# One kernel, another deal of side work: gate rounds 3-2-3, sums of magnitudes moved, weight-block sums split

## The chip, the core and the metric

The kernel runs on one core of a Trainium2 chip. The metric is the device time of one execution in microseconds (us). Five engines work side by side, each on its own in-order queue: TensorE (PE in the profile, with PEld for its weight loads) multiplies, VectorE (DVE), ScalarE (ACT) and GpSimd (POOL) do elementwise work, SyncE (SP) issues the DMAs. An instruction waits for semaphores of other engines, and all behind it on its queue wait with it.

## What is computed

Attention with a learned position bias, a gated feed-forward layer over its output, and then a layer of eight experts, whose part is the one that changes:

```python
def _moe2_ref(x, w_gate, w1, w2):           # x 1152x512, w1 8x512x1024, w2 8x1024x512
    logits = x @ w_gate
    P = np.exp(logits - logits.max())
    for _ in range(8):                       # the gate rounds
        P /= P.sum(1, keepdims=True) + 1e-09 # rows
        P /= P.sum(0, keepdims=True) + 1e-09 # columns
        P *= N / E
    for e in range(E):
        h = np.maximum(x @ w1[e], 0.0)       # first products
        out += P[:, e:e + 1] * (h @ w2[e])   # second products
```

## The kernel before

All products run in 16 bits with each operand split into a high and a low part; three products of parts make one. To split, a weight block is scaled by a power of two that comes from its largest magnitude ("sums of magnitudes", lines 754 on DVE and 102 on ACT; they go to DRAM and back, are read by line 751, and lines 727 to 836 make the power).

**First products.** `up(n, extra)` for n = 0 to 31, four blocks per expert, computes a block of `h` by seven products (x, z, y, x, y, x, z: the order of PSUM tiles, a Strassen-like scheme) of twelve matmuls each (line 1241). ACT copies a result out (`snap`, line 1251), DVE joins (lines 1255, 1300), ACT makes the high part of `h` (line 1259), DVE the low part (line 1264). Between the products are seven places, "segments" 0 to 6, where `then(seg)` runs side work that `between` or `extra` hold for (n, seg).

**Side work.** `prep(n, k)` makes weight block n ready for `up(n)`: step 0 scales (line 931, ACT), 1 and 2 make sums of blocks (lines 935, 936 and 939, 940, DVE), 3 and 4 the high parts (lines 943 and 947, ACT) and 3 and 5 the low parts (lines 944 and 950, POOL). `p2(e, i)` splits a row block of `w2[e]`: for e = 0, first four, lines 1032 (ACT) and 1033 (DVE), later lines 1035, 1036 (ACT) and 1037 (POOL). `pe(e, i)` takes one magnitude of expert e, `send` and `power` carry it on. `t4` makes sums of `w2` blocks (line 1325).

**Second products.** The first expert uses `down_0(h)`, once for each half of its `h` (after n = 2 and n = 4): nine tiles of 128 tokens, twelve matmuls each (line 1344), into `ps_d`, a PSUM pool of two buffers; `add` takes the result to `acc`, on ACT in the first half (line 1333), on DVE in the second (line 1335). Experts 1 to 7 use `down(e)` after their fourth block: half of tile 8, four rounds i = 0 to 3 on a pair of tiles each, by seven products of sums (lines 1419, 1424), the rest of tile 8. DVE makes the sums of `h` for the next round (line 1412) and accumulates (line 1335). Side work of a round stands in a table by (i, place); place 3 is ahead of the accumulations of `pz`, place 4 behind that of `py`.

**Gate.** `gate` takes the logits; `top` and `spread` find the largest and spread it to all lanes (`nmx`, line 1162), then ACT takes the exponential. A round is `rows` (lines 1169 to 1172, DVE) and `cols` (a matmul, line 1176, and lines 1177 to 1180 on DVE). The eight rounds lie in the first expert, one column sum after another.

The order is written out by hand: each engine's queue follows the order of calls in the program, and pools of buffers set the waits.

Of the kernel before, what the change touches and what calls it, by code (L numbers as in the profile page):

```python
# [52 lines left out]
def make_body(stop=None):  # L53
    def body(tc, a):
# [21 lines left out]
        with ctx, tc.manual_schedule():  # L76
# [146 lines left out]
            with ExitStack() as bctx:  # L223
# [180 lines left out]
                for g16 in range(NG16):  # L404
                    ps = bias_mm(g16)
                    t = bias_ev(g16, ps)
# [415 lines left out]
            def peak_all(name, items):  # L822

                items = [x for x in items if x[0] < 2 * NE]
                if items:
                    m = scl.tile([128, 2], F32, tag="pm", name="pm", bufs=2)[:, 0:len(items)]
                    peak_in(name, m)
                    peak_pow(m, items)
# [273 lines left out]
            with ExitStack() as ectx:  # L1102
# [44 lines left out]
                def gate():  # L1147
                    V.tensor_copy(out=P.rearrange("p t e -> p (t e)"), in_=pg[0][:, :NTT * NE])
                    mx = sk.tile([128, 1], F32, name="mx")
                    V.tensor_reduce(out=mx, in_=P, op=ALU.max, axis=AX.XY)  # L1150
                    nm = sk.tile([1, 1], F32, name="nm")
                    nmx = sk.tile([128, 1], F32, name="nmx")

                    def top():
                        pm = ps_d.tile([128, 512], F32, tag="d", name="pm")
                        T.transpose(pm[:1, :128], mx, ident)
                        V.tensor_reduce(out=nm, in_=pm[:1, :128], op=ALU.max, axis=AX.X, negate=True)

                    def spread():
                        pm2 = ps_d.tile([128, 512], F32, tag="d", name="pm2")  # L1160
                        T.matmul(out=pm2[:, 0:1], lhsT=ones[:1, :], rhs=nm, start=True, stop=True)
                        V.tensor_copy(out=nmx, in_=pm2[:, 0:1])
                        A.activation(out=P, in_=P, func=AF.Exp, bias=nmx)

                    between[2, 4].insert(0, top)
                    between[2, 6].append(spread)

                def rows():
                    V.tensor_reduce(out=row, in_=P, op=ALU.add, axis=AX.X)
# [25 lines left out]
                def m_spread():  # L1195
# [7 lines left out]

                between = {(0, 0): [m_top, end("t2"), end("h4")], (0, 1): [end("l4"), end("l2v"), end("tb")],
                           (0, 2): [end("t4"), end("h5"), end("l5")], (0, 3): [end("h6"), end("l6")],
                           (1, 5): [p2(0)], (2, 0): [lambda: peak_all(*SC), p2(1)], (2, 4): [p2(3)], (2, 5): [],
                           (1, 6): [logits], (2, 2): [flip], (2, 3): [gate, p2(2)], (1, 2): [lambda: peak_get(SC[0])],
                           (2, 6): []}
                kh_t = {}

# [157 lines left out]
                def down_0(h):  # L1368

                    parts = [(*h_t.pop(h), *w2t[0], 4 * h)]  # L1370
                    kh = kh_t.pop(h)
                    jp.append(sn)
                    if h == 0:
                        todo = {0: p2(0, 4) + pe(1, 1, 2, 3) + send(1, 1), 1: p2(0, 5), 2: prep(3, 1), 3: prep(3, 2, 3) + p2(0, 6),
                                4: p2(0, 7) + pe(1, 4, 5), 5: prep(3, 4, 5) + pe(1, 6), 6: power(1, 1) + prep(4, 0),
                                7: prep(4, 1, 3) + pe(1, 7), 8: prep(4, 2) + pe(1, 8, 9)}
                    else:
                        todo = {0: power(1, 2) + prep(5, 0), 1: prep(5, 1, 2) + p2(1, 0), 2: prep(5, 3) + p2(1, 1),
                                3: prep(5, 4, 5) + pe(2, 0) + p2(1, 2), 4: p2(1, 3) + prep(6, 0), 5: prep(6, 1) + p2(1, 4),
                                6: prep(6, 2, 3) + p2(1, 5), 7: pe(2, 1) + p2(1, 6) + pe(2, 4), 8: p2(1, 7) + pe(2, 5)}  # L1380
                    for t in range(NTT):
                        add(t, slice(0, DM), next(plain(t, parts)), kh, h, h == 0)
                        if h == 0 and t in (2, 4, 6, 8) or h == 1 and t in (0, 4):
                            cols(banks[0])
                        if t == 0 or h == 0 and t in (2, 4, 6, 8):
                            rows()
                        run(todo.get(t, ()))
                    jp.pop()

                def down(e):  # L1390
# [38 lines left out]
                    if e < NE - 1:  # L1429
                        put(0, 3, power(e + 1, 2) + [lambda: pace(e + 1)] + p2(e + 1, 0, 1, 2, 3))  # L1430
                        put(1, 0, power(e + 1, 1))
                        for i in range(3):
                            put(i + 1, 0, prep(4 * e + 4 + i, 0))
                            put(i + 1, 3, prep(4 * e + 4 + i, 1, 2, 4, 5, 3) + p2(e + 1, *((4,), (5,), (6, 7))[i]))
                        put(2, 1, pe(e + 2, 4, 5))
                        put(2, 2, pe(e + 2, 6, 7))
                        put(3, 1, pe(e + 2, 8))
# [58 lines left out]
                for n in range(4 * NE):  # L1496
                    e, q = divmod(n, 4)
                    extra = {}
                    put = lambda seg, fs: extra.setdefault(seg, []).extend(fs)
                    if n == 1:  # L1500
                        for seg, ks in ((0, (0,)), (1, (1, 2)), (2, (3,)), (3, (4, 5))):
                            put(seg, prep(2, *ks))
                    if n == 2:
                        put(3, prep(3, 0))
                    if n == 1:
                        put(6, pe(1, 0))
                    if n == 3:
                        put(0, prep(4, 4, 5) + pe(1, 10))
                        put(1, pe(1, 11))
                        put(2, send(1, 2))  # L1510
                    if n == 4:
                        for seg in (1, 5):
                            put(seg, [lambda: cols(ps_d)])
                            put(seg + 1, [rows])
                    if n in (2, 4):
                        put(3, [lambda h=n // 2 - 1: gains(h)])
                    if e and q == (1 if e == 1 else 0):
                        b_s = split_b(e)
                    t4 = lambda *ks: [b_s[k] for k in ks]
                    if n == 5:  # L1520
                        put(0, prep(6, 4, 5) + pe(2, 6))
                        put(1, pe(2, 2))
                        put(2, t4(0))
                        put(3, prep(7, 0))
                        put(4, prep(7, 1))
                        put(5, pe(2, 7))
                        put(6, prep(7, 2))
                    if n == 6:
                        put(0, prep(7, 3, 4, 5))
                        put(1, pe(2, 3))  # L1530
                        put(2, t4(1))
                        put(3, pe(2, 8, 9))
                        put(4, t4(2))
                        put(6, t4(3))
                    if n == 7:
                        put(0, pe(2, 10, 11) + t4(4))
                        put(1, [lambda: send_both(2)] + t4(5, 6))
                        put(2, t4(7))
                    if e > 1:
                        if q == 0:  # L1540
                            put(0, pe(e + 1, 9))
                            put(1, pe(e + 1, 0))
                            put(2, t4(0))
                            put(3, prep(n + 3, 0))
                            put(4, t4(1))
                            put(6, t4(2))
                        if q == 1:
                            put(0, prep(n + 2, 3) + pe(e + 1, 10))
                            put(1, pe(e + 1, 1))
                            put(2, prep(n + 2, 1))  # L1550
                            put(4, prep(n + 2, 2))
                            put(6, t4(3))
                        if q == 2:
                            put(0, prep(n + 1, 4, 5) + pe(e + 1, 11))
                            put(1, send(e + 1, 2) + pe(e + 1, 2))
                            put(2, t4(4))
                            put(4, t4(5))
                        if q == 3:
                            put(1, pe(e + 1, 3))
                            put(2, send(e + 1, 1) + t4(6))  # L1560
                            put(4, t4(7))
                    if e and q == 3:
                        put(4, [lambda: gains(e + 1)])
                    up(n, extra)
                    if n in (2, 4):
                        down_0(n // 2 - 1)
                    elif e and q == 3:
                        down(e)
# [61 lines left out]
```

## Time and profile before

| what | value |
|---|---|
| median of 3 runs | 1032.64 us (1032.63 to 1032.74) |
| the profiled execution: its time, its span | 1033.74 us, 1032.0 us |
| busy in the span: PE, DVE, ACT, POOL | 1016.0, 817.4, 610.4, 315.1 us |
| granted TensorE clock | 1.00 throughout |
| mean DMA rate | 82 GB/s |

The span runs from the first to the last instruction of the profiled execution, and times in the rows below are us from its start. The last products of the feed-forward layer end at about 333 us; up to 474 us lie the first expert and the blocks of the second, and from there each expert takes 85 us. In a timeline a bracket gives the idle time of the engine ahead of the row and what ended it.

### The profile page before, as it was taken

Reading aid. Unit: us, or ns where it says so; the run is one execution under the profiler, and the core shown is the slowest. Engines: PE = TensorE matmul, PEld = TensorE weight load, DVE = VectorE, ACT = ScalarE, POOL = GpSimd, SP = SyncE. Lnnn points to the kernel's source line nnn. Section 1 sums busy time; section 2 is a strip of 40 time slices with the busy share of each in tenths; the row PEclk is TensorE's granted clock in tenths of the full one; section 3 lists DMA queues with packets and bytes.
Section 4 is the critical chain, followed back from the end, with each engine's and each line's share of the span. In section 5 each row is a group of like instructions: output and inputs, shape, how many; then the busy total and the mean of one; then the engine's idle time right before and its main releaser. Section 6 shows DMA issues by size and latency. Waiting matters only on the chain.

```text
span 1032.0 us, 21993 instructions
## 1 busy us (share of the span) xinstructions
PE 1016.0 (98%) x8842; PEld 802.3 (78%) x8842; DVE 817.4 (79%) x1716; ACT 610.4 (59%) x1112; POOL 315.1 (31%) x224
## 2 busy tenths in 40 slices
PE   8999999999999999999999999999999999999998
PEld 3266777999999756478877877887887787787787
DVE  8977776899948886889878868868877886886784
ACT  9989887344326766665664565366466366535510
POOL 6951543232203102431420440341152053034100
PEclk9999999999999999999999999999999999999999
DMA  6985662433340111210310220220121022000001
GB/s 190 278 262 194 196 203 66 172 114 112 64 143 22 34 62 55 92 55 21 107 44 6 93 72 4 65 84 20 41 88 41 7 93 72 4 4 1 2 22 72
DMA packets 39891, 84.58 MB, mean 82 GB/s; under 512 B 8100, under 2 KB 10732, under 8 KB 39788
## 3 DMA queue, kind: packets, MB, share of 16 engines
q1 hardware_dynamic: 39788, 83.17, 25.3%
q8 instruction: 69, 1.13, 0.5%
q14 instruction: 34, 0.28, 0.2%
HBM read 69.86 MB, written 13.30 MB: 81 GB/s over the span
## 4 chain that ended last, share of the span: by engine, by line
PE 73%; DVE 9%; ACT 2%; issue 1%; DVEq 0%; ACTq 0%
PE x L1241 12%; PE m L602 11%; PE y L1241 8%; PE z L1241 8%; PE d L1344 7%; PE px L1419 6%; PE o L1079 4%; PE pz L1419 4%; PE py L1419 4%; PE pz L1424 4%; DVE s L1412 2%; PE px L1424 2%; PE py L1424 2%; DVE acc L1335 2%; DVE s L1255 1%; DVE hl L1264 1%
## 5 line engine op out<-in xcount | busy, mean ns | idle before, releaser
L1241 PEld LDWEIGHTS <-w1h 128*128 128x128 f16 x1792 | 175.0, 98 | 48.1 <-issue 2.9
L1259 ACT ACTIVATE hh<-s 128x576 f16<-128x576 f32 x128 | 87.1, 681 | 81.4 <-DVE s L1255 51.9
L1264 DVE SCALAR_TENSOR_TENSOR hl<-s,hh 128x576 f16<-128x576 f32 x128 | 98.6, 772 | 34.8 <-ACT hh L1259 31.3
L1037 POOL TENSOR_TENSOR w2l<-w2r,w2h 128x512 f16<-128x512 f32 x56 | 67.4, 1211 | 189.5 <-ACT w2h L1036 187.5
L950 POOL TENSOR_TENSOR w1l<-wf,w1h 128x1024 f16<-128x1024 f32 x32 | 68.3, 2134 | 148.1 <-issue 82.1
L1241 PEld LDWEIGHTS <-w1l 128*128 128x128 f16 x896 | 87.7, 98 | 22.1
L944 POOL TENSOR_TENSOR w1l<-wf,w1h 128x768 f16<-128x768 f32 x32 | 54.0, 1687 | 159.4 <-ACT w1h L943 118.4
L1419 PEld LDWEIGHTS <-s 128*128 128x128 f16 x896 | 87.6, 98 | 11.8 <-issue 1.7
L1424 PEld LDWEIGHTS <-hh 128*128 128x128 f16 x896 | 87.7, 98 | 10.2
L1251 ACT ACTIVATE s<-x,cx 128x576 f32<-128x576 f32 x96 | 70.5, 734 | 15.8 <-PE x L1241 15.2
L1335 DVE SCALAR_TENSOR_TENSOR acc<-px,kh,acc 128x256 f32<-128x256 f32 x112 | 52.8, 480 | 32.9 <-PE px L1419 28.3
L1241 PE MATMUL x<-xth,w1h 128*128 128x288 f16 x384 | 78.4, 286 | 0.1
L1241 PE MATMUL x<-xth,w1l 128*128 128x288 f16 x384 | 78.4, 286 | 0.0
L1241 PE MATMUL x<-xtl,w1h 128*128 128x288 f16 x384 | 78.4, 286 | 0.0
L602 PE MATMUL m<-xh,wh 128*128 128x384 f32 x216 | 73.3, 340 | 0.0
L602 PE MATMUL m<-xl,wh 128*128 128x384 f32 x216 | 73.0, 338 | 0.0
L602 PE MATMUL m<-xh,wl 128*128 128x384 f32 x216 | 73.0, 338 | 0.0
L1255 DVE SCALAR_TENSOR_TENSOR s<-z,cx,s 128x576 f32<-128x576 f32 x64 | 52.2, 816 | 22.1 <-PE z L1241 18.8
L494 DVE CUSTOM_DVE_ANT_0 ng<-sc,bias 128x576 f32<-128x576 f32 x72 | 51.6, 754 | 15.5 <-PE sc L481 6.9
L1035 ACT ACTIVATE w2r<-w2r,pc 128x512 f32<-128x512 f32 x48 | 34.0, 708 | 50.1 <-DVE pc L1021 50.1
L947 ACT ACTIVATE w1h<-wf 128x1024 f16<-128x1024 f32 x32 | 33.7, 1053 | 48.5 <-DVE wf L940 48.5
L1419 PE MATMUL px<-t,s 128*128 128x256 f16 x448 | 58.0, 272 | 0.6
(262 smaller groups left out, 2774.6 us busy)
## 6 DMA issues: line engine op xcount, KB each, us to landing
wr<-in_moe_w SPq DMA_DIRECT2D x50, 512.0 KB, 4.1
w2r<-in_moe_w SPq DMA_DIRECT2D x64, 256.0 KB, 2.7
bias_f<-bo SPq DMA_DIRECT2D x36, 295.5 KB, 4.4
bias<-bias_f SPq DMA_DIRECT2D x32, 288.0 KB, 4.4
qk<-in_qk SPq DMA_DIRECT2D x6, 576.0 KB, 4.8
wr<-in_moe_w_out SPq DMA_DIRECT2D x6, 512.0 KB, 3.3
v<-in_v SPq DMA_DIRECT2D x4, 640.0 KB, 5.0
bias<-bias_f SPq DMA_DIRECT2D x16, 144.0 KB, 4.7
```

What stands on the lines that cost most here:

```text
L602: T.matmul(out=p[:, :TG], lhsT=ws[:, 128 * c:128 * c + 128], rhs=xs[:, c, TG * g:TG * g + TG], start=(c == 0 and n == 0), stop=(c == 3 and ...
L950: G.tensor_tensor(out=lo[:, 3:7], in0=t[:, 4:8], in1=hi[:, 3:7], op=ALU.subtract)
L1037: G.tensor_tensor(out=lo, in0=r, in1=hi, op=ALU.subtract)
L1241: T.matmul(out=ps[bank][:, s, :SH], lhsT=ws[:, i, c, :], rhs=xv[:, j, c, s * SH:s * SH + SH], start=(start and k == 0), stop=(k == 5), **kw)
L1251: A.activation(out=t, in_=src, func=AF.Identity, scale=c)
L1255: V.scalar_tensor_tensor(out=out, in0=z, scalar=scale, in1=out, op0=ALU.mult, op1=ALU.add)
L1259: A.activation(out=o, in_=src, func=AF.Relu)
L1264: V.scalar_tensor_tensor(out=l, in0=src, scalar=0.0, in1=o, op0=ALU.max, op1=ALU.subtract)
L1335: V.scalar_tensor_tensor(out=o, in0=ps, scalar=s, in1=o, op0=ALU.mult, op1=ALU.add)
L1344: T.matmul(out=pd, lhsT=x, rhs=w, start=(y == 0), stop=(y == len(mm) - 1))
L1419: T.matmul(out=out, lhsT=x[z][:, j], rhs=w[z][:, j], start=(start and j == z == 0), stop=(j == 3 and z == 1), skip_group_check=True)
L1424: T.matmul(out=out, lhsT=(ha, hb)[j // 4][0][:, j % 4, 128 * t:128 * t + 128], rhs=wh[:, j, n], start=False, stop=(j == 7), skip_group_che ...
```

## The change

Only calls move; no instruction is added or taken away but for the place of some sums' scratch tile.

- `spread` moves from segment 6 of block 2 to segment 5, and `p2(0, 2)` from segment 3 to 4.
- Gate rounds: column sums at tiles 2, 4, 6 of the first half (before: 2, 4, 6, 8), two in block 4 as before, and at tiles 1, 4, 7 of the second half (before: 0, 4).
- `pe(1, 7)` to `pe(1, 11)` all stand in the first half's tiles 6 to 8; `prep(4, 3)` moves to block 3. In the second half `prep(5)`, `prep(6)`, `p2(1)` and `pe(2)` are spread otherwise over the tiles; in blocks 6 and 7 one `pe(2)` moves.
- `down(e)`, e = 1 to 6: of `prep`'s steps 1, 2, 4, 5, 3 at place 3 only step 1 stays; the others and `p2` move to place 4.

```diff
-                    between[2, 6].append(spread)
+                    between[2, 5].append(spread)
...
-                           (1, 5): [p2(0)], (2, 0): [lambda: peak_all(*SC), p2(1)], (2, 4): [p2(3)], (2, 5): [],
-                           (1, 6): [logits], (2, 2): [flip], (2, 3): [gate, p2(2)], (1, 2): [lambda: peak_get(SC[0])],
+                           (1, 5): [p2(0)], (2, 0): [lambda: peak_all(*SC), p2(1)], (2, 4): [p2(2), p2(3)], (2, 5): [],
+                           (1, 6): [logits], (2, 2): [flip], (2, 3): [gate], (1, 2): [lambda: peak_get(SC[0])],
...
-                                4: p2(0, 7) + pe(1, 4, 5), 5: prep(3, 4, 5) + pe(1, 6), 6: power(1, 1) + prep(4, 0),
-                                7: prep(4, 1, 3) + pe(1, 7), 8: prep(4, 2) + pe(1, 8, 9)}
+                                4: p2(0, 7) + pe(1, 4, 5), 5: prep(3, 4, 5) + pe(1, 6), 6: power(1, 1) + prep(4, 0) + pe(1, 7),
+                                7: prep(4, 1) + pe(1, 8, 9), 8: prep(4, 2) + pe(1, 10, 11)}
                     else:
-                        todo = {0: power(1, 2) + prep(5, 0), 1: prep(5, 1, 2) + p2(1, 0), 2: prep(5, 3) + p2(1, 1),
-                                3: prep(5, 4, 5) + pe(2, 0) + p2(1, 2), 4: p2(1, 3) + prep(6, 0), 5: prep(6, 1) + p2(1, 4),
-                                6: prep(6, 2, 3) + p2(1, 5), 7: pe(2, 1) + p2(1, 6) + pe(2, 4), 8: p2(1, 7) + pe(2, 5)}
+                        todo = {0: power(1, 2) + prep(5, 0), 1: p2(1, 0), 2: prep(5, 1, 2) + p2(1, 1),
+                                3: prep(5, 3) + pe(2, 0) + p2(1, 2), 4: prep(5, 4, 5) + p2(1, 3), 5: p2(1, 4) + prep(6, 0),
+                                6: prep(6, 1) + p2(1, 5) + pe(2, 4), 7: prep(6, 2) + p2(1, 6) + pe(2, 5),
+                                8: pe(2, 1) + prep(6, 3) + p2(1, 7)}
...
-                        if h == 0 and t in (2, 4, 6, 8) or h == 1 and t in (0, 4):
+                        if t in ((2, 4, 6), (1, 4, 7))[h]:
                             cols(banks[0])
-                        if t == 0 or h == 0 and t in (2, 4, 6, 8):
+                        if t in ((0, 2, 4, 6), (1, 4))[h]:
                             rows()
...
-                            put(i + 1, 3, prep(4 * e + 4 + i, 1, 2, 4, 5, 3) + p2(e + 1, *((4,), (5,), (6, 7))[i]))
+                            put(i + 1, 3, prep(4 * e + 4 + i, 1))
+                            put(i + 1, 4, prep(4 * e + 4 + i, 2, 4, 5, 3) + p2(e + 1, *((4,), (5,), (6, 7))[i]))
...
                     if n == 3:
-                        put(0, prep(4, 4, 5) + pe(1, 10))
-                        put(1, pe(1, 11))
-                        put(2, send(1, 2))
+                        put(0, prep(4, 3, 4, 5))
+                        put(1, send(1, 2))
...
-                        put(3, pe(2, 8, 9))
+                        put(3, pe(2, 8))
...
-                        put(0, pe(2, 10, 11) + t4(4))
+                        put(0, pe(2, 9, 10, 11) + t4(4))
```

What the calls become on the queues, at three places. First DVE at the end of block 2, from the largest logit on (`mx`, `nm` and `nmx` are the three steps of spreading it, `kh` a gain, `w2l` a low part of `w2`, `hl` a low part of `h`). Before:

```order
L1150 TENSOR_REDUCE mx<-P 128x1
L1033 SCALAR_TENSOR_TENSOR w2l<-w2r,pw,w2h 128x512
L1214 TENSOR_SCALAR kh<-pw,cx 128x1
L1215 TENSOR_SCALAR kh<-kh 128x1
L1255 SCALAR_TENSOR_TENSOR s_5782<-y,cx,s_5782 128x576
L1157 TENSOR_REDUCE nm<-pm 1x1
L1033 SCALAR_TENSOR_TENSOR w2l<-w2r,pw,w2h 128x512
L1264 SCALAR_TENSOR_TENSOR hl<-s_5782,hh 128x576
L1300 TENSOR_TENSOR s_5756<-s_5835,s_5756 128x576
L1255 SCALAR_TENSOR_TENSOR s_5835<-z,cx,s_5835 128x576
L1264 SCALAR_TENSOR_TENSOR hl<-s_5756,hh 128x576
L1264 SCALAR_TENSOR_TENSOR hl<-s_5835,hh 128x576
```

and behind these the copy of `nmx`. Now:

```order
L1150 TENSOR_REDUCE mx<-P 128x1
L1214 TENSOR_SCALAR kh<-pw,cx 128x1
L1215 TENSOR_SCALAR kh<-kh 128x1
L1255 SCALAR_TENSOR_TENSOR s_5782<-y,cx,s_5782 128x576
L1157 TENSOR_REDUCE nm<-pm 1x1
L1033 SCALAR_TENSOR_TENSOR w2l<-w2r,pw,w2h 128x512 x2
L1264 SCALAR_TENSOR_TENSOR hl<-s_5782,hh 128x576
L1300 TENSOR_TENSOR s_5756<-s_5835,s_5756 128x576
L1162 COPY nmx<-pm_5839 128x1
L1255 SCALAR_TENSOR_TENSOR s_5835<-z,cx,s_5835 128x576
L1264 SCALAR_TENSOR_TENSOR hl<-s_5756,hh 128x576
L1264 SCALAR_TENSOR_TENSOR hl<-s_5835,hh 128x576
```

The copy of `nmx` stands three steps earlier, and the first of two `w2l` steps behind `nm`.

Then ACT from the scaling of weight block 4 to block 3's copy of `y` (`junk` is a sum of magnitudes, `w1h` a high part of weights). Before:

```order
L931 ACTIVATE wf<-wr_5023,pw 128x1024
L1333 ACTIVATE acc<-d,kh 128x512
L943 ACTIVATE w1h<-wf 128x768
L102 ACTIVATE junk,pe<-w2r 128x512
L1333 ACTIVATE acc<-d,kh 128x512
L102 ACTIVATE junk,pe<-w2r 128x512 x2
L1251 ACTIVATE s_6108<-x,cx 128x576
L947 ACTIVATE w1h<-wf 128x1024
L102 ACTIVATE junk,pe<-w2r 128x512 x2
L1251 ACTIVATE s_6143<-y,cx 128x576
```

Now:

```order
L931 ACTIVATE wf<-wr_5023,pw 128x1024
L102 ACTIVATE junk,pe<-w2r 128x512
L1333 ACTIVATE acc<-d,kh 128x512
L102 ACTIVATE junk,pe<-w2r 128x512 x2
L1333 ACTIVATE acc<-d,kh 128x512
L102 ACTIVATE junk,pe<-w2r 128x512 x2
L1251 ACTIVATE s_6100<-x,cx 128x576
L943 ACTIVATE w1h<-wf 128x768
L947 ACTIVATE w1h<-wf 128x1024
L1251 ACTIVATE s_6139<-y,cx 128x576
```

The same steps, with the five sums all ahead of the copy of `x` and the two high parts together behind it.

Last, DVE at the turn from round 1 to round 2 of `down(2)`, the same in every `down(e)` up to e = 6 (`wf` is a weight block, `pz`, `py` and `px` are products). Before:

```order
L935 TENSOR_TENSOR wf<-wf 128x256
L936 TENSOR_TENSOR wf<-wf 128x256
L939 TENSOR_TENSOR wf<-wf 128x256
L940 TENSOR_TENSOR wf<-wf 128x256
L1335 SCALAR_TENSOR_TENSOR acc<-pz,kh,acc 128x256 x2
L1335 SCALAR_TENSOR_TENSOR acc<-py,kh,acc 128x256
L1335 SCALAR_TENSOR_TENSOR acc<-px,kh,acc 128x256 x2
```

Now:

```order
L935 TENSOR_TENSOR wf<-wf 128x256
L936 TENSOR_TENSOR wf<-wf 128x256
L1335 SCALAR_TENSOR_TENSOR acc<-pz,kh,acc 128x256 x2
L1335 SCALAR_TENSOR_TENSOR acc<-py,kh,acc 128x256
L939 TENSOR_TENSOR wf<-wf 128x256
L940 TENSOR_TENSOR wf<-wf 128x256
L1335 SCALAR_TENSOR_TENSOR acc<-px,kh,acc 128x256 x2
```

Lines 939 and 940 stand behind three accumulations instead of ahead of them.

## Rows read from the trace of the kernel before

**Rows 1.** The page, busy us (share of the span) and instructions.
```profile
PE 1016.0 (98%) x8842; PEld 802.3 (78%) x8842; DVE 817.4 (79%) x1716; ACT 610.4 (59%) x1112; POOL 315.1 (31%) x224
```
**Rows 2.** Busy time by stretch: window, length, each engine's busy us, clock, DMA.
```profile
800.00:900.00 100.00, 99.85 (x832) 81.22 (x831) 81.53 (x162) 55.31 (x88) 24.47 (x16) 1.00 0.15 45
```
**Rows 3.** Timeline of TensorE, first expert: start, us, engine, line, instruction [idle before].
```profile
372.80 0.38 PE L1344 MATMUL d<-w2h,hh 128*128 128x512 f16 x1 [1.66 <-DVE nmx L1162]
...
401.61 0.40 PE L1241 MATMUL y<-xth,w1h 128*128 128x288 f16 x2 [1.36 <-ACT s L1251]
...
406.02 0.41 PE L1241 MATMUL x<-xth,w1h 128*128 128x288 f16 x2
...
421.18 0.41 PE L1176 MATMUL pc<-P,ones 128*128 128x72 f32 x2 [1.77 <-DVE P L1172]
```
**Rows 4.** Timeline of TensorE, fourth round of `down(2)`.
```profile
592.70 0.27 PE L1419 MATMUL py<-tx,s 128*128 128x256 f16 x1
593.08 0.49 PE L1419 MATMUL px<-t,s 128*128 128x256 f16 x3
```
**Rows 5.** Timeline of DVE, end of block 2.
```profile
369.49 0.75 DVE L1300 TENSOR_TENSOR s<-s,s 128x576 f32<-128x576 f32 x1
...
372.59 0.15 DVE L1162 COPY nmx<-pm 128x1 f32<-128x1 f32 x1
```
**Rows 6.** Timeline of ACT, end of the first half and block 3.
```profile
392.51 1.15 ACT L931 ACTIVATE wf<-wr,pw 128x1024 f32<-128x1024 f32 x1 [2.94 <-DVE pw L836]
...
398.65 1.06 ACT L947 ACTIVATE w1h<-wf 128x1024 f16<-128x1024 f32 x1 [0.50 <-DVE wf L940]
...
400.84 0.72 ACT L1251 ACTIVATE s<-y,cx 128x576 f32<-128x576 f32 x1
```
**Rows 7.** Timelines of POOL, DVE and ACT in block 3.
```profile
399.79 2.12 POOL L950 TENSOR_TENSOR w1l<-wf,w1h 128x1024 f16<-128x1024 f32 x1 [3.04 <-ACT w1h L947]
...
402.17 0.76 DVE L1264 SCALAR_TENSOR_TENSOR hl<-s,hh 128x576 f16<-128x576 f32 x1 [2.82 <-ACT hh L1259]
...
404.80 0.72 ACT L1251 ACTIVATE s<-x,cx 128x576 f32<-128x576 f32 x1
```
**Rows 8.** Timelines of POOL and DVE in block 6, one step of each.
```profile
457.68 2.14 POOL L950 TENSOR_TENSOR w1l<-wf,w1h 128x1024 f16<-128x1024 f32 x1
...
458.63 1.80 DVE L1264 SCALAR_TENSOR_TENSOR hl<-s,hh 128x576 f16<-128x576 f32 x1 [0.61 <-ACT hh L1259]
```
**Rows 9.** Timeline of DVE, two steps of column rounds.
```profile
389.32 0.83 DVE L1178 TENSOR_SCALAR col<-col 128x8 f32<-128x8 f32 x1
...
433.41 0.90 DVE L1180 SCALAR_TENSOR_TENSOR P<-P,col 128x72 f32<-128x72 f32 x1
```
**Rows 10.** The chain that ended last: two tiles of second products.
```profile
378.31 5.18 PE d L1344 x24
```
**Rows 11.** Timelines of DVE and ACT, rounds 1 to 3 of `down(2)`.
```profile
580.23 0.42 DVE L940 TENSOR_TENSOR wf<-wf 128x256 f32<-128x256 f32 x1
580.68 1.06 ACT L947 ACTIVATE w1h<-wf 128x1024 f16<-128x1024 f32 x1 [4.57 <-DVE wf L940]
...
584.67 1.21 DVE L1412 TENSOR_TENSOR s<-hh 128x512 f16<-128x512 f16 x1
585.81 1.38 DVE L1412 TENSOR_TENSOR s<-hl 128x512 f16<-128x512 f16 x1
587.12 0.41 DVE L1412 TENSOR_TENSOR s<-s,hh 128x512 f16<-128x512 f16 x1
...
592.16 0.87 DVE L1335 SCALAR_TENSOR_TENSOR acc<-px,kh,acc 128x256 f32<-128x256 f32 x2
```
**Rows 12.** Timeline of POOL, the same stretch.
```profile
581.87 2.14 POOL L950 TENSOR_TENSOR w1l<-wf,w1h 128x1024 f16<-128x1024 f32 x1 [5.37 <-issue]
583.97 1.64 POOL L944 TENSOR_TENSOR w1l<-wf,w1h 128x768 f16<-128x768 f32 x1
585.56 1.35 POOL L1037 TENSOR_TENSOR w2l<-w2r,w2h 128x512 f16<-128x512 f32 x1
```

## Prediction

> **What bounds the kernel now.** TensorE is busy for 1016.0 of 1032.0 us [rows 1], and in a late stretch it leaves 0.15 of 100 us idle [rows 2], at full clock. So work on the other engines is free until TensorE waits for it, and the question is only which waits of TensorE go and which come. I read the shares of the page first, then the table by stretch, then TensorE's own timeline, where a bracket gives the idle time ahead of a row, and last the queues of VectorE (DVE), ScalarE (ACT) and GpSimd (POOL) at those places.
>
> The first expert has three waits [rows 3]: 1.66 us ahead of tile 1 of the first half's second products (for `nmx`), 1.36 us in the first products of block 3 (for ACT's copy of `y`), and 1.77 us ahead of the second half's first column sum (for the row step of `P`). That is 4.79 us, the most that this part of the change can win. Later one small wait comes back in every `down(e)` from e = 1 to 6, in its fourth round: the last matmul into `py` starts at 592.70 and the first into `px` at 593.08, 0.38 us later, where such matmuls start 0.11 us apart (three in 0.49 us, the last of them 0.27 long) [rows 4]. So 0.27 us are lost, six times, 1.6 us in all.
>
> **First wait: gone.** `nmx` is a copy of 0.15 us that stands on DVE behind a join and two low parts; the add that it has to follow by data starts at 369.49 us, the copy at 372.59 us [rows 5]. In the changed order it follows that add at once, so it ends at about 370.3 us, while TensorE asks for the PSUM buffer at about 371.1. Slack 0.8 us: 1.66 us are won. The two splits of weight rows (line 1033) that now come later are covered too: they end some 1 us before the third and fourth quarter of tile 0 read them.
>
> **Second wait: nearly all stays.** What makes ACT late is the scaling of weight block 4 (line 931), for which ACT sat idle 2.94 us until the power was known [rows 6]. That power hangs on the gate round at tile 6, and its DVE steps come 1.6 us earlier now, so line 931 starts at about 390.9 us. From its start to the copy of `y` ACT took 400.84 - 392.51 = 8.33 us [rows 6]. The sums of magnitudes and the high parts are dealt otherwise between these two points, but they are the same five and two; only the 0.50 us of waiting for DVE ahead of line 947 goes, since tile 8 has no gate round any more. So the copy starts at 390.9 + 7.8 = 398.7 to 398.8, and TensorE goes on at about 399.6. Without any wait it would be there at 401.61 - 1.66 - 1.36 - 0.17 (a column sum that now comes later) = 398.4. So about 1.2 of the 1.36 us stay, in two pieces, the first of them ahead of the third product, since all five sums now stand before the first copy. I count 0.2 us won.
>
> **A new wait behind it.** ACT's two high parts of block 4 now stand back to back, so POOL's two low parts run from about 398.1 to 401.85, the longer one ending when it did before [rows 7]; the low part of `h` on DVE (line 1264), which came at 402.17 after POOL was through, now comes at 400.2 and falls into it. What that means the trace shows elsewhere: with POOL's line 950 on from 457.68 to 459.82, the same DVE step took 1.80 us and ended 0.6 us after POOL [rows 8], against 0.76 us when free [rows 7]. So it ends at 402.5 instead of 400.95; behind it stand DVE's join, ACT's high part and ACT's copy of `x`, which ended 0.5 us before TensorE began the next block at 406.02 in the old order [rows 3, 7] and now ends 0.6 us late (404.6 for 404.0), and then the join that frees `z`, 0.3 us late. Cost 0.9 us. Bounds: nothing if the step slips in ahead of POOL; 1.5 us if none of the slack is there.
>
> **Third wait: replaced by others.** The second half's first tile now has no gate round, so 1.77 us go. But its rounds fall on tiles 1, 4 and 7, two of them with row sums behind, while POOL is busy with weight parts of 1.2 to 2.1 us one behind the other. Steps of DVE that read two operands from SBUF, and small scalar steps, stand still while a POOL step runs: 0.83 us for a scalar step on 8 numbers a lane, 0.90 us for the last step of a column round [rows 9], 1.2 and 1.4 us for sums that take 0.41 [rows 11]. After each POOL step one DVE step gets through. A tile of TensorE takes 5.18 / 2 = 2.59 us [rows 10], and DVE must have added tile t before tile t + 2 may start. Laying the rows' durations end to end along the three queues (the same addition gives the old order's end of this half within 0.15 us), the round at tile 1 loses 0.7 + 0.8 us to POOL and the weight sums behind it 0.8 + 0.8, so tile 3 is added 0.95 us too late for tile 5; the round at tile 4 makes tile 7 wait 0.9. Sum 1.9 us, against 1.77 that go: 0.1 us lost. That the two small steps of a row sum (lines 1170, 1172) are held too is the weak point, as no row of the trace has them beside a POOL step; if they are not, 0.7 us of waiting are left and 1.1 us are won. I take them as held, since the scalar step of line 1178 and the two-operand sums of line 1412 are [rows 9, 11]. The Trainium skill ("SBUF — State Buffer", section "Who interferes with whom") says that a VectorE step with two SBUF inputs is blocked by a GpSimd step that reads SBUF, and one with at most one input and no two-port mode is not; by that rule line 1172 is held and line 1170 may not be, which would put the sum between the two values. No row here decides it.
>
> **The split of the weight sums in the later experts.** This is the largest term. Only the order changes: two of the four sums (lines 939, 940) move behind three accumulations. In round 2 (the third) of `down(2)` DVE has no gap from 584.67 to the end of the accumulation at 592.16 (+0.87) that lets `px` go on [rows 11], so the order alone wins nothing there. But ACT's high part (line 947) starts 0.03 us after line 940 ends, and POOL's three steps follow it: 581.87, 583.97, 585.56, the last ending at 586.91 [rows 12]. With 940 behind three accumulations of 0.39 us, they start 1.17 us later, the first running until 585.15. DVE's sums for the next round begin at 584.67. In the old order two of them were held, 1.21 and 1.38 us long for 0.41, and the third was free at 587.12 [rows 11]. In the new one the first is held to 585.4 by line 950, the second to 587.2 by line 944, the third to 588.5 by line 1037: the third ends 1.0 us later than 587.53. Nothing on DVE behind it is idle, so the accumulation ends at 594.0, and the 0.27 us become 1.28. Rounds 1 and 3 have slack: there DVE waits for TensorE. So 1.01 us in each of six experts: 6.1 us lost. Bounds: 1.6 us won, if the three sums slip past POOL and the old wait goes too; 9 us lost, if POOL's three steps run without letting DVE in.
>
> **Sum.** -1.66 - 0.2 + 0.9 + 0.1 + 6.1 = +5.2 us. Against the profiled execution (1033.74 us, a span of 1032.0 and 1.74 around it) that is 1038.9; the median of the runs shown is 1.1 us lower, so 1032.64 + 5.2 gives **1037.8 us**, with 1036.0 to 1039.5 for this case alone.
>
> **Rivals.** *POOL holds DVE less than I take it to.* Then the step in block 3, the gate rounds and the three sums all get through; the first expert wins most of its 4.79 us and the later ones lose nothing: 1032.64 - 4.8 = 1027.8, **faster**. It is decided at the first sum after 584.67: 0.4 us long or over 0.7. Against it stand the held steps of 0.8 to 1.8 us [rows 8, 9, 11]; for it, that I have no row with DVE waiting for line 950 and two more POOL steps queued. *The late sums are not reached*, since ACT and POOL move less than 1.17 us: then only the first expert's -0.9 counts, 1031.7, no change. *The first expert keeps nearly all its gain*, as DVE catches up between the rounds, and the late loss stands: -4.4 + 6.1, about 1034.3, at the edge between no change and slower. *More is held*: a fourth sum in each `down`, or the round at tile 7 as well: about 1040.
>
> **Chances.** A measurement of this kernel can tell 0.2%, 2.1 us, from no change. Forecast 0.50; POOL holds less 0.18; late sums not reached 0.11; first expert keeps its gain 0.15, of which 0.09 within the bound and 0.06 beyond; more held 0.06. Faster 0.18, same 0.11 + 0.09 = 0.20, slower 0.50 + 0.06 + 0.06 = 0.62. The range leaves out the fast case and takes in the others: 1031.4 to 1040.0.
>
> **What would show it.** Right: no idle bracket ahead of tile 1; in blocks 3 and 4 three or four waits of 0.3 to 0.9 us; in the second half two waits of about 0.9 ahead of tiles 5 and 7; in each `down` three of DVE's sums at 0.7, 1.8 and 1.4 us instead of two, and a step of some 1.4 us from `py` to `px` in the fourth round. Wrong: that step at 0.4 us or less, which would take away the main term; or waits of over 2 us in the second half.

## The result, and the profile after

| | before | after |
|---|---|---|
| median of the runs, us | 1032.68 (1032.63 to 1032.74) | 1038.36 (1037.90 to 1038.85) |
| profiled execution, us (span) | 1033.74 (1032.0) | 1038.44 (1036.7) |
| TensorE busy, us | 1016.0 [rows 1] | 1016.6 |
| ratio after / before | | 1.0055, 95% interval 1.0038 to 1.0072 |

The change costs 5.7 us. The two profiled executions are only 4.7 us apart, since the old one was 0.7 us slower up to the first expert: the same matmul starts at 335.85 us there and at 335.15 us after the change. Times of the first expert are to be compared with that shift; in `down(2)` the two axes agree within 0.1 us. TensorE computes as long as before; what grew is its waiting. The trace's list of TensorE's waits from 330 us on says for what: engine, tile and line that waited, the tile and line it waited for, us in total, times, the longest. After the change:

```profile
PE px L1425 <- DVE acc L1335: 3.2, 6, 0.5
PE px L1420 <- DVE acc L1335: 2.6, 6, 0.4
PE d L1344 <- DVE acc L1335: 1.7, 2, 0.9
PE x L1241 <- ACT s L1251: 1.5, 2, 1.1
PE y L1241 <- ACT s L1251: 0.7, 1, 0.7
```

Two of the three single waits of before [rows 3] are gone from it, the one for `nmx` and the one for the row step of `P`, and the one for `y` is 0.7 us instead of 1.4. New are four in the first expert, two for `x` and two ahead of `d` (1.5 and 1.7 us in the list), and two that come back in each of six `down(e)`. (From here on, lines from 1412 on have numbers one higher in the changed kernel: line 1413 is the token sum that was 1412, line 1420 the product in `prod`, line 1425 that in `main`.)

TensorE's timeline after the change, first expert. The bracket is the idle time ahead of the row; the time lost, from one matmul's start to the next less the usual step, is about 0.16 us more than the bracket:

```profile
397.17 0.41 PE L1241 MATMUL x<-xth,w1h 128*128 128x288 f16 x2 [1.08 <-ACT s L1251]
...
399.48 0.41 PE L1241 MATMUL y<-xth,w1h 128*128 128x288 f16 x2 [0.68 <-ACT s L1251]
...
404.45 0.40 PE L1241 MATMUL x<-xth,w1h 128*128 128x288 f16 x2 [0.40 <-ACT s L1251]
...
429.78 0.38 PE L1344 MATMUL d<-w2h,hh 128*128 128x512 f16 x1 [0.95 <-DVE acc L1335]
...
435.86 0.38 PE L1344 MATMUL d<-w2h,hh 128*128 128x512 f16 x1 [0.74 <-DVE acc L1335]
```

With a smaller loss of 0.29 us at 406.20, which has no bracket, the first expert loses 1.24 + 0.85 + 0.57 + 0.29 + 1.12 + 0.91 = 4.98 us, against 1.82 + 1.52 + 1.93 = 5.27 before. By the traces this part of the change won 0.3 us.

Rounds 1 to 3 of `down(2)` after the change, first VectorE (DVE), then GpSimd (POOL), which answer to [rows 11, 12], and last TensorE, which answers to [rows 4]:

```profile
581.31 0.42 DVE L940 TENSOR_TENSOR wf<-wf 128x256 f32<-128x256 f32 x1
...
584.58 0.79 DVE L1413 TENSOR_TENSOR s<-hh 128x512 f16<-128x512 f16 x1
585.29 1.86 DVE L1413 TENSOR_TENSOR s<-hl 128x512 f16<-128x512 f16 x1
587.08 1.38 DVE L1413 TENSOR_TENSOR s<-s,hh 128x512 f16<-128x512 f16 x1
588.38 0.41 DVE L1413 TENSOR_TENSOR s<-s,hl 128x512 f16<-128x512 f16 x1
```

```profile
582.96 2.13 POOL L950 TENSOR_TENSOR w1l<-wf,w1h 128x1024 f16<-128x1024 f32 x1 [6.55 <-issue]
585.04 1.83 POOL L944 TENSOR_TENSOR w1l<-wf,w1h 128x768 f16<-128x768 f32 x1
586.83 1.34 POOL L1037 TENSOR_TENSOR w2l<-w2r,w2h 128x512 f16<-128x512 f32 x1
```

```profile
589.91 1.03 PE L1425 MATMUL px<-w2h,hh 128*128 128x256 f16 x8 [0.53 <-DVE acc L1335]
...
593.29 0.27 PE L1420 MATMUL py<-tx,s 128*128 128x256 f16 x1
594.00 0.49 PE L1420 MATMUL px<-t,s 128*128 128x256 f16 x3 [0.44 <-DVE acc L1335]
```

Line 940 ends 1.1 us later, POOL starts 1.1 us later (582.96 for 581.87), and three sums are held instead of two: they take 0.79, 1.86 and 1.38 us for 0.41. Each held sum ends 0.28 us behind a POOL step: 585.37 behind 585.09, 587.15 behind 586.87, 588.46 behind 588.17. TensorE loses 0.69 us at 589.91 and, from 593.29 to 594.00 less 0.11, 0.60 us more: 1.29 per `down`, where it was 0.27. Six times 1.02 is 6.1 us. With -0.3 in the first expert that makes +5.8 for the +5.7 measured.

### The profile page after: what moved, and what is told of

The parts are those of the page before. It is cut to its first block, busy times and chain, and to the rows that moved or that the text cites. A ratio compares the mean times of both kernels' runs of the same rounds, so it can differ in the third digit from the quotient of the medians.

```text
span 1036.7 us, 21997 instructions
## 1 busy us (share of the span) xinstructions
PE 1016.6 (98%) x8842; PEld 802.2 (77%) x8842; DVE 823.9 (79%) x1716; ACT 609.4 (59%) x1112; POOL 316.0 (30%) x224
## 4 chain that ended last, share of the span: by engine, by line
PE 69%; DVE 11%; ACT 2%; DMA 1%; issue 1%; DVEq 0%; ACTq 0%
PE x L1241 11%; PE m L602 11%; PE y L1241 8%; PE z L1241 8%; PE px L1420 6%; PE d L1344 4%; PE o L1079 4%; PE py L1420 4%; PE pz L1420 4%; PE pz L1425 4%; DVE s L1413 3%; DVE acc L1335 2%; PE py L1425 2%; PE px L1425 2%; DVE hl L1264 1%; DVE s L1255 1%
```

## The experiments

The theory: what the change does to the order of operations matters only through POOL, whose steps hold DVE's; the later experts lose 6 us since POOL starts 1.1 us later there, and the first expert comes out about even. The rivals: the loss sits in the first expert; the new order costs by itself, whatever POOL does. Each kernel is compared with the kernel before on the same chip, whose median was 1032.62 to 1032.69 us each time.

**1 and 2. The change cut in two.** `split_only` is the old kernel with this alone, `first_only` the changed kernel without it:

```diff
-                            put(i + 1, 3, prep(4 * e + 4 + i, 1, 2, 4, 5, 3) + p2(e + 1, *((4,), (5,), (6, 7))[i]))
+                            put(i + 1, 3, prep(4 * e + 4 + i, 1))
+                            put(i + 1, 4, prep(4 * e + 4 + i, 2, 4, 5, 3) + p2(e + 1, *((4,), (5,), (6, 7))[i]))
```

> The old kernel with only the later experts' weight sums split (two of four behind three accumulations). Theory of the record: six times 1.0 us, so 1032.7 + 6.0 = 1038.7 us, and the three held sums of 0.8, 1.9 and 1.4 us in each down(e). Rival (the loss comes from the first expert's new order): 1032.7 us, no change.

> The changed kernel with the later experts' weight sums put back into one piece. Theory: the late waits fall from 7.8 us to 1.95 and what is left is the first expert's own balance, -0.3 to -0.9 us: 1031.7 to 1032.5 us. Rival (the first expert lost the time): 1036 us or more.

`split_only`: 1038.62 us, ratio 1.0057 (1.0045 to 1.0070). `first_only`: 1032.01 us, 0.9994 (0.9985 to 1.0003). So the later split is the whole loss: alone it costs 5.9 us, and the first expert's part alone cannot be told from no change. The list of waits of `split_only` has the two late waits beside the old ones (that for `y`, 1.1 us there, is not shown):

```profile
PE px L1424 <- DVE acc L1335: 3.2, 6, 0.5
PE px L1419 <- DVE acc L1335: 2.7, 6, 0.4
PE pc L1176 <- DVE P L1172: 1.8, 1, 1.8
PE d L1344 <- DVE nmx L1162: 1.7, 1, 1.7
```

**3 and 4. The dose.** The same four sums, in one piece as in the old kernel, at two other places of the round: `early` ahead of the last two token sums, `later` behind the last accumulation.

```diff
-                            put(i + 1, 3, prep(4 * e + 4 + i, 1, 2, 4, 5, 3) + p2(e + 1, *((4,), (5,), (6, 7))[i]))
+                            put(i + 1, 5, prep(4 * e + 4 + i, 1, 2, 4, 5, 3) + p2(e + 1, *((4,), (5,), (6, 7))[i]))
...
                         add(i + 4, n1, x, kh, h)
+                        more(i, 5)
                         run(nxt[3])
```

(that is `early`; in `later`, `more(i, 5)` stands at the end of the round, behind `out(i + 4)`)

> The old kernel with the four weight sums and what follows them put before the last two token sums of the round, so that ACT and POOL start about 0.67 us earlier and no operation is added or removed. Theory (POOL's last step holds VectorE's second sum, and the chain behind it makes TensorE wait 0.27 us per down): the third sum starts near 586.45 on the old time axis instead of 587.12, the 0.27 us go in all six experts, 1032.7 - 1.6 = 1031.1 us. Rival (the order of VectorE's own steps sets the wait, POOL's place is without effect): 1032.7 us.

> The old kernel with all four weight sums and what follows them at the end of the round, behind four accumulations. Theory: POOL's three steps start about 0.45 us later than in the changed kernel, the third held sum ends 0.4 us later, so 0.4 us more per down than the split costs: 1038.7 + 2.5 = 1041.2 us. Rival (the split costs because it cuts the sums in two, not because POOL starts later): the sums are in one piece here, 1032.7 us.

`early`: 1031.15 us, 0.9985 (0.9976 to 0.9994). `later`: 1045.27 us, 1.0122 (1.0108 to 1.0136). DVE's timeline in `down(2)`, the first three token sums of the third round, of `early`:

```profile
584.18 0.54 DVE L1412 TENSOR_TENSOR s<-hh 128x512 f16<-128x512 f16 x1
584.65 1.38 DVE L1412 TENSOR_TENSOR s<-hl 128x512 f16<-128x512 f16 x1
585.95 0.41 DVE L1412 TENSOR_TENSOR s<-s,hh 128x512 f16<-128x512 f16 x1
```

and of `later`, and behind them, from TensorE's timeline, the matmul that waited longest there:

```profile
585.44 1.68 DVE L1412 TENSOR_TENSOR s<-hh 128x512 f16<-128x512 f16 x1
587.05 1.86 DVE L1412 TENSOR_TENSOR s<-hl 128x512 f16<-128x512 f16 x1
588.83 1.38 DVE L1412 TENSOR_TENSOR s<-s,hh 128x512 f16<-128x512 f16 x1
```

```profile
591.66 0.60 PE L1424 MATMUL px<-w2h,hh 128*128 128x256 f16 x4 [1.42 <-DVE acc L1335]
```

POOL's line 950 starts at 580.71 in `early` and at 584.71 in `later`. Counted against the start of the first token sum, the four kernels line up:

| | POOL ahead of the first sum, us | the three sums take, us | lost per `down`, us | time, us |
|---|---|---|---|---|
| `early` | 3.47 | 0.54, 1.38, 0.41 | none | 1031.15 |
| before | 2.80 | 1.21, 1.38, 0.41 | 0.27 | 1032.69 |
| `split_only` | 1.63 | 0.79, 1.86, 1.38 | 1.29 | 1038.62 |
| `later` | 0.73 | 1.68, 1.86, 1.38 | 2.45 | 1045.27 |

In `early` even the old wait goes. The rival of `later` falls: its sums are in one piece and it is the slowest. My own figure for it was too small, 2.5 us above the split where 6.65 were measured: I placed POOL 0.45 us later than in the changed kernel, and it was 0.9 by the table, as the last accumulation itself waits 0.39 us for TensorE. The cost per `down` in `later` is 1.58 us at the third round's end, 0.61 in the fourth and 0.26 in the next block.

**5. POOL out of the way.** `no_low` is the changed kernel with POOL's three subtractions (lines 944, 950, 1037) replaced by writes of zero from the third expert's weights on, so it leaves out those low parts. One of the three:

```diff
-                        G.tensor_tensor(out=lo[:, 3:7], in0=t[:, 4:8], in1=hi[:, 3:7], op=ALU.subtract)
+                        G.memset(lo[:, 3:7], 0.0)
```

> The changed kernel in which GpSimd, from the weights of the third expert on, writes zeros into the three low parts of weights instead of subtracting (part of the computation left out: these low parts are zero). VectorE, ScalarE and TensorE keep every operation and their order. Theory (GpSimd's steps that read SBUF hold VectorE's sums): the sums take 0.41 us each and all 7.8 us of late waits go, 1038.4 - 7.8 = 1030.6 us. Rival (the later place of the weight sums on VectorE alone makes the waits): 1038.4 us. Between: if writing alone holds VectorE as well, 1032 to 1036 us with sums of over 0.41 us.

1030.30 us, 0.9976 (0.9967 to 0.9985). The writes of zero wait for no sum and no high part, only for their buffers, so the last of them ends at 559.92 us, some 23 us ahead of the sums below, and POOL is idle in these rounds. With the same order on DVE and ScalarE (ACT) as in the changed kernel, the sums take

```profile
582.98 0.41 DVE L1422 TENSOR_TENSOR s<-hh 128x512 f16<-128x512 f16 x1
583.31 0.42 DVE L1422 TENSOR_TENSOR s<-hl 128x512 f16<-128x512 f16 x1
583.64 0.42 DVE L1422 TENSOR_TENSOR s<-s,hh 128x512 f16<-128x512 f16 x1
```

(line 1422 there is line 1413 of the changed kernel), and no late wait is left in the list. So it is POOL, and not the order on DVE. Whether a POOL step that only writes holds DVE too isn't told by these sums, as none stood beside them; another place of the same trace tells it for a step with two operands, the low part of `h` (line 1273 there), first beside a subtraction, then beside a write:

```profile
456.24 2.14 POOL L956 TENSOR_TENSOR w1l<-wf,w1h 128x1024 f16<-128x1024 f32 x1
...
461.07 0.74 POOL L945 MEMSET w1l<- 128x768 f16 x1
```

```profile
457.20 1.79 DVE L1273 SCALAR_TENSOR_TENSOR hl<-s,hh 128x576 f16<-128x576 f32 x1 [0.50 <-ACT hh L1268]
...
461.08 0.76 DVE L1273 SCALAR_TENSOR_TENSOR hl<-s,hh 128x576 f16<-128x576 f32 x1 [0.15 <-ACT hh L1268]
```

It takes 1.79 us beside the subtraction and its usual 0.76 beside the write. A scalar step on 8 numbers was held by a write, in the one place where a trace has the two side by side: in the next run line 1187 takes 0.46 us instead of 0.17, from 417.00 us, beside a write from 416.69 to 417.43.

**6. The same in the first expert's second half.** `no_low_half2` has the later sums in one piece and POOL's subtractions replaced, as above, from the second half's preparations on.

> The changed kernel with the later weight sums in one piece as before, and GpSimd writing zeros instead of subtracting in all low parts of weights that are prepared from the first expert's second half on (part of the computation left out). Theory (GpSimd's steps hold the rounds' small steps and the weight sums, lines 1170, 1172, 1178 and 935 to 940): the waits of 1.1 and 0.9 us ahead of tiles 5 and 7 go, and the late 1.6 us with them: 1032.0 - 2.0 - 1.6 = 1028.4 us, lines 1170 and 1172 at 0.2 us each. Rival (three rounds and the weight sums are simply too much for VectorE in that half): the waits ahead of tiles 5 and 7 stay, 1030.4 us.

1028.12 us, 0.9955 (0.9942 to 0.9969). From 417 us on its list of waits is empty: the waits ahead of tiles 5 and 7 are gone, with three column rounds and every weight sum where the change put them. The two steps of a row round, first of the changed kernel, then of this one (whose lines 1179 and 1181 they are):

```profile
422.97 0.88 DVE L1170 TENSOR_SCALAR row<-row 128x9 f32<-128x9 f32 x1
...
424.13 1.05 DVE L1172 TENSOR_TENSOR P<-P,row 128x72 f32<-128x72 f32 x1
```

```profile
424.29 0.17 DVE L1179 TENSOR_SCALAR row<-row 128x9 f32<-128x9 f32 x1
...
424.75 0.23 DVE L1181 TENSOR_TENSOR P<-P,row 128x72 f32<-128x72 f32 x1
```

**7. The gate's spread alone.** `spread_only` is the old kernel with the first two pieces of the diff:

```diff
-                    between[2, 6].append(spread)
+                    between[2, 5].append(spread)
...
-                           (1, 5): [p2(0)], (2, 0): [lambda: peak_all(*SC), p2(1)], (2, 4): [p2(3)], (2, 5): [],
-                           (1, 6): [logits], (2, 2): [flip], (2, 3): [gate, p2(2)], (1, 2): [lambda: peak_get(SC[0])],
+                           (1, 5): [p2(0)], (2, 0): [lambda: peak_all(*SC), p2(1)], (2, 4): [p2(2), p2(3)], (2, 5): [],
+                           (1, 6): [logits], (2, 2): [flip], (2, 3): [gate], (1, 2): [lambda: peak_get(SC[0])],
```

> The old kernel with only the gate's spread one segment earlier (and one split of weight rows one segment later). Theory: the first wait of 1.66 us goes and the power, ScalarE and the copy of y move with it, so the second and third waits keep their length: 1032.7 - 1.7 = 1031.0 us. Rival (what is won is waited for again ahead of block 3's y or the second half's first column sum): 1032.7 us, with a bracket of about 3 us at one of these places.

1031.13 us, 0.9985 (0.9976 to 0.9994). The wait for `nmx` is gone. Of the other two, one did not keep its length, and a new reason is in the trace: first TensorE's list, then DVE's row for the power of weight block 4.

```profile
PE pc L1176 <- DVE P L1172: 1.8, 1, 1.8
PE y L1241 <- ACT s L1251: 1.3, 1, 1.3
PE x L1241 <- ACT s L1251: 0.4, 1, 0.4
```

```profile
391.17 0.29 DVE L751 TENSOR_REDUCE pm<-all 128x1 f32<-128x128 f32 x1 [1.02 <-DMA all<-peakse]
```

DVE is ready for line 751 some 1.5 us earlier (the row step ahead of it ends at 390.15 us, in the old kernel at 391.65), and now stands 1.02 us for the transfer that brings the gathered peaks; in the old kernel it waited for nothing there. Block 3 lost 1.52 us before and loses 0.61 + 1.48 = 2.09 here. So of the 1.8 us that were won, 0.6 come back. By the traces that is 1.25 us; the measured 1.5 +- 0.9 cannot tell it from 1.7.

**8 to 12. What the same reasons give if they are used.** `spread_early` joins the moves of `spread_only` and `early`; `spread_early_2_6` is that with the second half's column rounds moved from tiles 0 and 4 to 2 and 6, and its row step from 0 to 2; `block4_rounds` is `spread_early` with block 4's second round one segment earlier; `sums_moved` is `spread_early` with three of ACT's sums of magnitudes moved behind the third copy of block 3; `all_moved` has both of these last two pieces, which are

```diff
-                                 7: prep(4, 1, 3) + pe(1, 7), 8: prep(4, 2) + pe(1, 8, 9)}
+                                 7: prep(4, 1, 3) + pe(1, 7), 8: prep(4, 2) + pe(1, 8)}
...
-                        put(0, prep(4, 4, 5) + pe(1, 10))
-                        put(1, pe(1, 11))
-                        put(2, send(1, 2))
+                        put(0, prep(4, 4, 5))
+                        put(3, pe(1, 9, 10))
+                        put(5, pe(1, 11))
+                        put(6, send(1, 2))
...
-                        for seg in (1, 5):
+                        for seg in (1, 4):
```

> The old kernel with the spread one segment earlier and the weight sums of the later experts ahead of the last two token sums. Theory: two separate waits, so the gains add: 1032.7 - 1.7 - 1.6 = 1029.4 us. Rival (the first is waited for again later): 1031.1 us.

> As the one before, and the second half's two column rounds at tiles 2 and 6 instead of 0 and 4, its row step at tile 2 instead of 0. Theory: the third wait of 1.8 us goes, since the rows of P are ready by then, and GpSimd's steps hold the small steps of the round for 0.3 to 1.1 us in its place: 1029.4 - 0.7 to 1.5 = 1027.9 to 1028.7 us. Rival (the round lands amid the weight parts and is held as long as in the changed kernel, 2 us): 1029.4 us or more.

> The old kernel with the spread earlier and the later weight sums early (1029.5 us), and block 4's second column round and its row step one segment earlier, ahead of a join and two low parts. Theory: the rows of P are ready when the second half's first column sum asks for them, the third wait of 1.8 us goes: 1029.5 - 1.8 = 1027.7 us. Rival (VectorE's backlog stays and tile 0 is added too late for tile 2): 1029.5 us with a wait of 1 to 2 us ahead of tile 2.

> The old kernel with the spread earlier and the later weight sums early (1029.5 us), and three of ScalarE's five sums of magnitudes in block 3's first products moved behind its third copy. Theory (those sums of 0.6 us make the copies of x and y late): both waits of block 3, 0.4 and 1.3 us, go: 1029.5 - 1.7 = 1027.8 us; or 1028.7 us if the high parts, now earlier, set GpSimd on VectorE's low part of h and cost 0.9 us in block 4. Rival (the copies wait for the power, not for the sums): 1029.5 us.

> All four moves together. Theory: the waits are separate, 1032.7 - 1.7 - 1.6 - 1.8 - 0.8 to 1.7 = 1025.9 to 1026.8 us. Rival (what is won in block 3 is waited for in the second half): 1027.7 us.

| | us | ratio to before (95%) |
|---|---|---|
| `spread_early` | 1029.53 | 0.9971 (0.9959 to 0.9982) |
| `spread_early_2_6` | 1031.11 | 0.9982 (0.9973 to 0.9991) |
| `block4_rounds` | 1028.87 | 0.9960 (0.9947 to 0.9972) |
| `sums_moved` | 1028.31 | 0.9958 (0.9945 to 0.9970) |
| `all_moved` | 1026.58 | 0.9943 (0.9930 to 0.9955) |

`spread_early_2_6` is a miss, as its rival had it: the round falls amid POOL's steps as in the changed kernel. Three of its small steps, POOL's steps beside them, and what TensorE then did:

```profile
425.88 1.73 DVE L1170 TENSOR_SCALAR row<-row 128x9 f32<-128x9 f32 x1
427.64 0.22 DVE L1171 RECIPROCAL row<-row 128x9 f32<-128x9 f32 x1
427.89 0.89 DVE L1172 TENSOR_TENSOR P<-P,row 128x72 f32<-128x72 f32 x1
```

```profile
425.45 2.12 POOL L950 TENSOR_TENSOR w1l<-wf,w1h 128x1024 f16<-128x1024 f32 x1
427.54 2.27 POOL L1037 TENSOR_TENSOR w2l<-w2r,w2h 128x512 f16<-128x512 f32 x2
```

```profile
429.49 0.38 PE L1344 MATMUL d<-w2h,hh 128*128 128x512 f16 x1 [2.09 <-DVE acc L1335]
```

The scalar step (line 1170) ends 0.04 us behind the POOL step beside it (427.61 and 427.57), where it takes 0.17 us alone; the reciprocal (line 1171) runs its usual 0.22 us although POOL is busy.

`block4_rounds` puts the round where POOL is idle, and its list of waits has none for the row step; 0.29 us are lost ahead of the round's column sum, which is asked for earlier. By that trace (1027.66 us) the theory's 1027.7 holds; its median is 1.2 us above, with two of five executions near 1027.6 and three near 1029.1, and as only one was traced, that difference stays open. `sums_moved` wins 1.2 us over `spread_early`: the wait for `x` is gone, so that copy was late because of ACT's sums, and of the 1.49 us ahead of `y` 0.85 stay; the power still waits 0.94 us for its transfer there. `all_moved` keeps one wait in TensorE's list from 330 us on,

```profile
PE y L1241 <- ACT s L1251: 0.3, 1, 0.3
```

and beats the old kernel by 6.0 us and the changed one by 11.8.

## Why the prediction was right, and where it was not

The forecast was 1037.8 us, the result 1038.36. Term by term:

| term of the sum | predicted, us | measured, us |
|---|---|---|
| first wait | -1.66 | -1.82 by the trace |
| second wait | -0.2 | +0.57 (2.09 for 1.52) |
| new wait behind it | +0.9 | +0.86 (0.57 + 0.29) |
| third wait replaced | +0.1 | +0.10 (2.03 for 1.93) |
| split of the weight sums | +6.1 | +6.1 (six times 1.02); alone 5.9 |
| sum | +5.2 | +5.8 by the traces, +5.7 measured |

- **First wait.** Right; `nmx` is copied at 369.31 us and TensorE has no gap ahead of tile 1.
- **Second wait: the step that failed.** "That power hangs on the gate round at tile 6" was true of the old kernel alone. The round's DVE steps did come earlier, its last row step ends at 389.13 us in the changed kernel, but the power also hangs on a transfer, to which the sum gave no time (DVE's row, and ACT's scaling behind it):

```profile
389.91 0.29 DVE L751 TENSOR_REDUCE pm<-all 128x1 f32<-128x128 f32 x1 [0.78 <-DMA all<-peakse]
...
390.85 1.15 ACT L931 ACTIVATE wf<-wr,pw 128x1024 f32<-128x1024 f32 x1 [3.80 <-DVE pw L836]
```

  In the old kernel line 751 started 0.08 us ahead of the row step's end (391.57 and 391.65); so here it came 0.85 us late, and ACT's line 931 with it. The transfer had been issued 5.76 us ahead of that row (at 384.15 us), and in the old kernel 5.90 us (at 385.67): there it had landed by then and did not show as a wait. Without the delay, by an estimate, the two pieces would add up to 2.09 - 0.85 = 1.24 us, the 1.2 that I had. That line 931 starts at 390.85 us, where I had forecast 390.9, is luck: on the old trace's axis that is 391.55. The two pieces and their order were as predicted.
- **The new wait in blocks 3 and 4.** Right in place and size: the low part of `h` fell into line 950 (399.58 to 401.71) and took 2.29 us, from 400.03, instead of 0.76 [rows 7].
- **Third wait.** Right: 0.95 and 0.74 us of idle time ahead of tiles 5 and 7, forecast 0.95 and 0.9. The weak point is settled: lines 1170 and 1172 are both held, take 0.88 and 1.05 us, and run in 0.17 and 0.23 once POOL is out of the way (run 6). The Trainium skill ("SBUF — State Buffer", section "Who interferes with whom") counts single-input scalar steps among those that can take both ports and then contend with GpSimd; I had gone by its sentence on one-input steps alone. The traces agree with the wider reading, by those 0.88 us.
- **The split.** Right in mechanism and size. The sums were forecast at 0.7, 1.8 and 1.4 us and took 0.79, 1.86 and 1.38. Only the place was half right: I put all 1.28 us at `px` in the fourth round, but 0.69 of them fall at the third round's last products, which wait for the accumulation that stands behind the held sums; 0.60 are left for the fourth. So the step from `py` to `px` there is 0.71 us, neither the 1.4 that I gave as a sign nor the 0.4 that would have spoken against it.
- **Rivals.** "POOL holds DVE less" was decided where the text said, at the first sum: 0.79 us, not 0.4. "The late sums are not reached" falls by the same rows: POOL starts 1.1 us later. "The first expert keeps nearly all its gain" falls too: it kept 0.3 us of 5.27 by the traces, and `first_only` gives 0.6 +- 0.9. "More is held" did not come in `down`: the fourth sum takes 0.41 us, at 588.38.

## What to carry to other kernels

Moving work on one engine moves what that work releases on others: here two short sums behind three accumulations shifted 5 us of GpSimd work by 1.1 us, onto the VectorE steps that TensorE waits for, and cost 1 us in each of six experts. So follow a moved step through to the engine that starts when it ends, and ask what will then run beside it; put what feeds GpSimd early in a round, and short chains that TensorE waits for where GpSimd is idle. A step that now comes earlier only helps until the next thing it needs: look for the transfer or the engine that was hidden behind it, even where the trace shows no wait for it.

## What was not expected of the hardware

The wait of 2.09 us in `spread_early_2_6` was followed by a second loss. TensorE's granted clock in the next 3.5 us was 0.53, so about the 1.2 GHz level; the column is the one behind POOL's in the busy time by stretch, here 427 to 429.5 us and 429.5 to 433:

```profile
427.00:429.50 2.50, 0.41 (x3) 0.10 (x2) 2.43 (x5) 1.86 (x3) 2.50 (x3) 1.00 0.21 82
429.50:433.00 3.50, 3.50 (x9) 1.25 (x9) 1.72 (x2) 3.44 (x6) 3.20 (x4) 0.53 0.78 245
```

Matmuls that start 0.215 us apart elsewhere start 0.43 apart there, for some 8 of them: 1.6 us. The executions of that kernel show it as well: the eight with a mean granted clock of 0.997 or 0.998 took 1031.0 to 1031.8 us, the three with 0.999 or 1.000 took 1029.4 to 1030.4. Waits of 1.77 us at most [rows 3] left no such mark in the old kernel's trace. That the wait made the clock fall is read from the order in time; no run tests it by itself.
